# Order of splits, loads and buffers where an expansion hands over to a contraction

## The chip, the cores and the metric

The kernel runs on one core of a Trainium2 chip. Its engines have instruction queues of their own and meet through semaphores: TensorE (PE, matmuls; PEld, its weight loads), VectorE (DVE), ScalarE (ACT), GpSimd (POOL) and SyncE (SP), which here issues nearly all DMAs. The metric is the device time in microseconds of one execution.

## The reference

Linear attention with random features over 4 × 8 heads (576 tokens, 64 wide, 128 features), then two feed-forward layers on 2304 tokens of width 512:

```python
x = attention(q, k, v, omega)        # (2304, 512)
h = x @ w_in                         # 512 -> 2048
x = silu(h) @ w_out                  # 2048 -> 512
g = silu(x @ w_gate) * (x @ w_val)   # 512 -> 1536
out = g @ w_out2                     # 1536 -> 512
```

Inputs are float32, the weights are stored as float64 and converted on the chip.

## The kernel before

After the attention come four phases: up 1 (x @ w_in), down 1 (@ w_out), up 2 (gate and val), down 2. Each is a 2 × 2 block multiplication with seven products instead of eight, always in the order 1, 5, 6, 2, 7, 3, 4: the weight's quarters and their sums (A11, S1, S2, ...) against the activation's quarters and their differences (B11, T1, T2, B21, T3, B22, T4). A float32 operand is split into a high part of the matmul's type and a low part, and three matmuls (high·high, high·low, low·high) stand for one. ScalarE copies the high part, VectorE subtracts it for the low one.

An up phase runs in steps n (24 in up 1, 36 in up 2); a product of a step is 6 matmuls of 128 × 128 × 384 (L1103). ScalarE moves results between PSUM banks (L1120) and applies SiLU (L1144), VectorE adds (L1177), SyncE stores each 128 × 384 result in the DRAM tile g_d (L1129). A down phase runs over 3 blocks s of 768 tokens, seven products p and pieces k (4 in down 1, 3 in down 2); a piece is 12 matmuls (L1478). Below, (s,p,k) is such a piece.

For each piece the quarter of g is loaded by SyncE (L1311; B21 and B22 into `ra`, where up 1's weights lie, B11 and B12 into `fa`), ScalarE writes its high part (L1337), VectorE its low part (L1341), and for products 1, 5, 6 and 2 VectorE also makes the next difference in place (L1361): T1 = B12 − B11, T2 = B22 − T1, T3 = B22 − B12, T4 = B21 − T2. High and low part each take one buffer of 768 columns from the list `f_z`. In down 1 the list holds four cut from `ra` by `open_z` and one more (`gap`, given when down 1 begins); a piece's two come back when its matmuls are recorded. `open_z` may run once the weights in w_slots 4 and 5 are done with; that is so from the end of step 21 on. B21's place is that of weight slots 0 and 1, B22's that of 2 and 3; up 1's last step, 23, uses slots 2 and 3.

Down 1's weights were converted earlier and lie in DRAM (`wd_out`). For each product two or three weight pieces are loaded (L1282), ScalarE takes the high part (L1286), VectorE the low one (L1290). Pieces for products 1, 5, 6 and 2 and two of product 7 go to `ra` and `rb` while up 1 runs; product 7's last one and those of 3 and 4 go to `rc`, whose places are up 1's activations of the last block, free at its end.

The order on every engine is made when the program is built. A planner keeps a clock for each engine with its own costs, and `flush` puts urgent operations (those of the running products) first; then it takes, of several streams, the operation with the earliest start. A stream's place in the dictionary `streams` adds 0.1 us a place to that start, so it breaks near ties: `z` (loads of quarters), `wd` (weights of a down phase), `split` (a down phase's operands), `x`, `conv` (conversion of weights). `z_first(m, ...)` lists the first block's loads in the order of the names it is given.

Of the kernel before, what the change touches and what calls it, by code (L numbers as in the profile page):

```python
# [42 lines left out]
def kernel(  # L43
# [57 lines left out]
    def cut(t, o, n):  # L101
        return t[:, o : o + n]
# [43 lines left out]
    def cost(kind, n):  # L146
        a, b = fixed[kind]
        return a + b * n
# [46 lines left out]
    class Stream:  # L195
# [30 lines left out]

    streams = {
        "z": Stream(0.2),
        "wd": Stream(1.0),
        "split": Stream(1.0),  # L230
        "x": Stream(1.2, DVE=3),
        "conv": Stream(1.5, ACT=2),
    }
# [28 lines left out]
    def drain(*some):  # L262

        ready = [(o.ready(), None, o) for o in urgent]
        ready = [x for x in ready if x[0] is not None]
        for st in some or streams.values():
            o = st.best(1e9)
            if o is not None:
                ready.append((max(o.ready(), clk[o.eng]), st, o))
        if not ready:  # L270
            return False
        _, st, o = min(ready, key=lambda x: x[0])
        if st is None:
            urgent.remove(o)
            o.emit()
        else:
            st.emit(o)
        return True
# [33 lines left out]
    f_c = Free("c", [cut(fa, C_AT + i * 512, 512) for i in range(3)])  # L312
# [5 lines left out]
    w_slots = [x for x, _ in f_w.q]  # L318
    W = {}

    def conv_job(kind, i, dram=None, side=False):
        b = {}
        key = lambda *k: (kind, i, *k)
# [13 lines left out]
        def word(h, w):  # L337
            return b["r", h].bitcast(U32).rearrange("p (c w) -> p c w", w=2)[:, :, w]

        def first(h):  # L340
            def go():
                b["c", h] = c = f_c.take()

                nc.scalar.activation(c, word(h, 1).bitcast(F32), AF.Prelu, scale=2.0**-112, alpha=-(2.0**32))  # L349

            return Op("ACT", cost("ACT", 512), go, ins=[key("r", h)], outs=[key("c", h)], slots=(f_c, 1))

        def shift(h):
            def go():
# [84 lines left out]
        def store(a, z, src, ins):  # L439
# [11 lines left out]
            return Op("SP", dma_cost(P * (z - a) * 1024), go, ins=[key(*x) for x in ins], outs=[key("d", a)])  # L451

        half = [load(0), load(1), first(0), first(1), shift(0), low(0), shift(1), low(1)]
        if dram is not None:
            return [
# [50 lines left out]
    def down_job(m, i):  # L506
        k = DNK[m]
        return conv_job(
            k, i, dram=lambda a, z: wd_d[k][a:z, :, i * 256 : (i + 1) * 256].rearrange("o p c -> p o c")
        )  # L510

    def up_job_dram(k):
        return conv_job(k, 0, dram=lambda a, z: wu_d[k][:, a * 256 : z * 256])
# [386 lines left out]
    for t in spare_c:  # L900
        f_c.give(t, 0.0)
    f_sum.give(spare_sum, 0.0)
    early["conv"].extend(chain(*(conv_job("in", i, side=True) for i in range(3)), *(down_job(0, i) for i in range(3))))
    early["x"].extend(x_prep(0, 0, xr1, False, "POOL", early=True))
    def two_steps(d):
# [81 lines left out]
    for f, some in ((f_c, spare_c), (f_sum, [spare_sum])):  # L987
        n = len(f.q)
# [316 lines left out]
    def zload(m, s, n, k, after=()):  # L1305
        fp = FP[m]
        a, h = HB[n]
        f = a * fp + 2 * k

        def go():  # L1310
            nc.sync.dma_start(  # L1311
                out=ZP[n](768 * k, 768).rearrange("p (f n) -> p f n", f=2).bitcast(F32),
                in_=g_d[m][s, h, f : f + 2].rearrange("f p n -> p f n"),
            )

        return Op(
            "SP", dma_cost(2 * P * N * 4), go, ins=[("g", m, s, h, f), ("g", m, s, h, f + 1), *after], outs=[("z", m, s, n, k)],
            guard=lambda: not len(streams["conv"]),
        )
# [190 lines left out]
    def up_order(kinds, n, head, tail):  # L1510
        pairs = [(i,) for i in range(n)]
        if head:
            pairs[:3] = [(0, 1, 2)]
        if tail:
            pairs[-3:] = [(n - 3, n - 2, n - 1)]
        return [(i, k, s) for ps_ in pairs for s in range(NSB) for i in ps_ for k in kinds]
# [16 lines left out]
    def more():  # L1533

        f_c.give(extra_c)
        f_raw.give(extra_raw)
# [5 lines left out]
    seq1 = up_order(("in",), FP[0], True, True)  # L1542
# [3 lines left out]
    def z_first(m, *names):  # L1546
        return [zload(m, 0, n, k) for n in names for k in range(FP[m] // 2)]

    def open_z():

        n = len(f_w.q)
        f_w.q = deque(x for x in f_w.q if not any(x[0] is t for t in w_slots[4:]))
        assert len(f_w.q) == n - 2
        for i in range(4):
            f_z.give(cut(ra, 7424 + i * 768, 768))
# [12 lines left out]
    def hook1(n, p):  # L1568
        if n == 0 and p == CONV_P:
            streams["conv"].extend(conv1)  # L1570
        if not len(streams["x"]) and not to_come and not opened:
            opened.append(True)
            more()
        if n == len(seq1) - 6 and p == 1:
            streams["wd"].extend(wd_ops)
        if n == len(seq1) - 1 and p == 1:
            open_z()
        if n == len(seq1) - 5 and p == 1:
            streams["z"].extend(z_first(0, "B11", "B12"))
            streams["split"].extend(next(d1))  # L1580

    up_phase(0, seq1, hook1)
    while len(streams["conv"]):
        assert drain()
    assert not to_come
    streams["z"].extend(z_first(0, "B21", "B22"))

    raw2_t = []

# [54 lines left out]
    up_phase(1, seq2, hook2)  # L1644
    while len(streams["conv"]):
        assert drain()
    streams["z"].extend(z_first(1, "B21", "B22"))
    open_z()
    for _ in d2:
        pass  # L1650
# [48 lines left out]
```

## Time and profile before

| | |
|---|---|
| three runs, median (lowest to highest) | 852.97 us (851.78 to 855.28) |
| profiled execution, own time | 853.52 us |
| its span | 851.7 us |
| TensorE matmul, weight load busy | 823.9, 796.4 us |
| VectorE, ScalarE, GpSimd busy | 623.8, 552.5, 164.8 us |
| up 1 ends, down 1's first matmul | 291.9, 293.3 us |
| up 2 ends, down 2's first matmul | 722.2, 722.2 us |

Times in rows count from the span's start. A timeline merges neighbours of one line: start, length, engine, line, operation, output<-input, count, and in brackets how long the engine had been idle before it and what it waited for. A row's length reaches to the end of its last instruction; matmuls overlap, so n of them in a row take less than n times the length of one.

### The profile page before, as it was taken

How to read it: one execution, taken by the hardware profiler on the slowest of the kernel's cores; microseconds unless marked ns; L12 is line 12 of the kernel's file. 1: busy time of each engine (PE TensorE's matmuls, PEld its weight loads, DVE VectorE, ACT ScalarE, POOL GpSimd, SP SyncE). 2: the span in 40 equal slices, each digit the busy share in tenths (PEclk: the TensorE clock that was granted, in tenths of full speed). 3: DMA queues.
4: the chain of work that ended last, by engine and by line, in shares of the span. 5: the costliest groups of instructions: out<-in, count | busy, mean ns of one | idle time of the engine just before them, and what ended most of it. 6: DMA issues, size and time to landing. Idle time of an engine off the chain costs nothing.

```text
span 851.7 us, 18196 instructions
## 1 busy us (share of the span) xinstructions
PE 823.9 (97%) x6889; PEld 796.4 (93%) x6889; DVE 623.8 (73%) x1016; ACT 552.5 (65%) x1166; POOL 164.8 (19%) x204
## 2 busy tenths in 40 slices
PE   8999999999999879999998998999999999999998
PEld 7888889999899879999998998999999999899998
DVE  4888877576644687796899998584757548979783
ACT  6999878776767854455557874655556557646552
POOL 0477831044440000000000035121213010000000
PEclk9999999999999999999999999999999999999999
DMA  8579866588999865608514657462637168483602
GB/s 284 183 259 299 282 211 226 173 260 282 333 310 364 286 231 165 206 22 243 181 62 141 218 179 208 146 204 100 211 97 238 53 212 283 169 272 94 220 3 75
DMA packets 110120, 170.09 MB, mean 200 GB/s; under 512 B 9424, under 2 KB 94032, under 8 KB 110032
## 3 DMA queue, kind: packets, MB, share of 16 engines
q1 hardware_dynamic: 109808, 168.69, 60.9%
q8 instruction: 54, 0.88, 0.4%
q14 instruction: 34, 0.28, 0.1%
q10 hardware_dynamic: 224, 0.23, 0.1%
HBM read 107.02 MB, written 61.87 MB: 198 GB/s over the span
## 4 chain that ended last, share of the span: by engine, by line
PE 76%; DVE 7%; DMA 7%; issue 4%; ACT 3%; POOL 2%; SPq 0%; DVEq 0%; ACTq 0%; POOLq 0%
PE ps L1103 36%; PE ps L1478 29%; PE ps L757 4%; PE ps L801 2%; PE ps L817 2%; DMA wd_out<-fa 2%; PE ps L848 2%; DMA ra<-g_d 2%; POOL fa L382 2%; DVE fa L363 1%; DMA fa<-in_moe_w_val 1%; DVE ra L1341 1%; DMA fa<-in_moe_w_out 1%; DVE ra L429 1%; PE ps L873 1%
## 5 line engine op out<-in xcount | busy, mean ns | idle before, releaser
L382 POOL TENSOR_TENSOR fa<-fa 128x256 f32<-128x256 f32 x124 | 105.6, 866 | 506.4 <-ACT fa L1144 239.3
L1103 PE MATMUL ps<-ra 128*128 128x384 f32 x840 | 148.4, 328 | 6.1 <-ACT ps L1120 4.0
L1103 PE MATMUL ps<-rb,ra 128*128 128x384 f32 x840 | 146.3, 327 | 2.1 <-ACT ps L1120 2.1
L1103 PE MATMUL ps<-rc,ra 128*128 128x384 f32 x840 | 145.8, 326 | 1.5 <-ACT ps L1120 1.5
L1103 PEld LDWEIGHTS ps<-ra 128*128 128x128 f32 x840 | 137.6, 189 | 9.0 <-ACT ps L1120 5.8
L1103 PEld LDWEIGHTS ps<-rb,ra 128*128 128x128 f32 x840 | 137.6, 189 | 3.6 <-ACT ps L1120 3.3
L1103 PEld LDWEIGHTS ps<-rc,ra 128*128 128x128 f32 x840 | 137.8, 189 | 2.5 <-ACT ps L1120 2.4
L1120 ACT ACTIVATE ps<-ps 128x384 f32<-128x384 f32 x180 | 85.4, 477 | 67.7 <-PE ps L1103 63.4
L1177 DVE TENSOR_TENSOR fa<-fa,ps 128x384 f32<-128x384 f32 x120 | 66.2, 551 | 80.5 <-ACT ps L1120 58.0
L1337 ACT ACTIVATE ra<-fa 128x768 fp32r<-128x768 f32 x86 | 71.9, 841 | 60.4 <-PE ps L1478 43.9
L1341 DVE TENSOR_TENSOR ra<-fa,ra 128x768 fp32r<-128x768 f32 x81 | 77.4, 955 | 21.6 <-PE ps L1478 13.4
L1478 PE MATMUL ps<-ra 128*128 128x384 f32 x486 | 84.0, 332 | 6.8 <-DVE ra L1341 5.7
L1478 PE MATMUL ps<-ra,rb 128*128 128x384 f32 x516 | 89.9, 327 | 0.4 <-DVE ra L1341 0.4
L1478 PEld LDWEIGHTS ps<-ra 128*128 128x128 f32 x486 | 80.7, 192 | 9.0 <-DVE ra L1341 7.4
L1478 PE MATMUL ps<-ra,rc 128*128 128x384 f32 x482 | 83.9, 327 | 2.2 <-DVE ra L1341 2.2
L1478 PEld LDWEIGHTS ps<-ra,rb 128*128 128x128 f32 x516 | 84.5, 189 | 1.4 <-DVE ra L1341 1.0
L773 ACT ACTIVATE kq<-ps,nb 128x128 f32<-128x128 f32 x288 | 79.3, 401 | 7.8 <-DVE nb L771 7.5
L1478 PEld LDWEIGHTS ps<-ra,rc 128*128 128x128 f32 x482 | 78.9, 189 | 3.4 <-DVE ra L1341 3.2
L349 ACT ACTIVATE fa<-fa 128x512 f32<-128x512 f32 x65 | 54.0, 833 | 20.2 <-DMA fa<-in_moe_w_in 5.7
L1361 DVE TENSOR_TENSOR fa<-ra,fa 128x768 f32<-128x768 f32 x63 | 60.0, 953 | 4.4 <-DMA ra<-g_d 3.7
L1144 ACT ACTIVATE fa<-fa 128x384 f32<-128x384 f32 x84 | 43.6, 519 | 25.5 <-DVE fa L1177 25.2
L363 DVE SCALAR_TENSOR_TENSOR fa<-fa 128x512 uint32<-128x512 uint32 x65 | 56.0, 862 | 0.7
(112 smaller groups left out, 1104.5 us busy)
## 6 DMA issues: line engine op xcount, KB each, us to landing
g_d<-fa SPq DMA_DIRECT2D x168, 192.0 KB, 4.1
fa<-g_d SPq DMA_DIRECT2D x42, 384.0 KB, 5.0
ra<-g_d SPq DMA_DIRECT2D x42, 384.0 KB, 4.3
fa<-in_moe_w_out SPq DMA_DIRECT2D x28, 512.0 KB, 5.1
fa<-in_moe_w_in SPq DMA_DIRECT2D x16, 512.0 KB, 5.0
wd_out<-fa SPq DMA_DIRECT2D x12, 512.0 KB, 3.2
fa<-in_moe_w_gate SPq DMA_DIRECT2D x12, 512.0 KB, 4.0
fa<-in_moe_w_val SPq DMA_DIRECT2D x12, 512.0 KB, 5.2
```

The lines of the kernel that those rows point to most:

```text
L349: nc.scalar.activation(c, word(h, 1).bitcast(F32), AF.Prelu, scale=2.0**-112, alpha=-(2.0**32))
L363: nc.vector.scalar_tensor_tensor(c, word(h, 0), 29, c, op0=ALU.logical_shift_right, op1=ALU.bitwise_or)
L382: f(blk(f"S{n}"), blk(l), blk(r))
L773: nc.scalar.activation(e[:, g // 2, g % 2, h * M : (h + 1) * M], x[:, g, :], AF.Exp, bias=nb[:, g : g + 1])
L1103: nc.tensor.matmul(woven(ps[b][:, :N]), cut(l, j * P, P), halves(cut(r, j * N, N)), start=start and c == 0, stop=stop and c == 5, skip_gro ...
L1120: nc.scalar.activation(out() if callable(out) else out, src, AF.Copy)
L1144: nc.scalar.activation(b["t"], src, AF.Silu)
L1177: nc.vector.tensor_add(t, t if in_place else p5[n], ps[bank_][:, :N])
L1337: nc.scalar.activation(ops[s, p, k][0], src(), AF.Copy)
L1341: nc.vector.tensor_sub(l, src(), h.bitcast(F32))
L1361: (nc.gpsimd if eng == "POOL" else nc.vector).tensor_sub(z(PLACE[to]), z(PLACE.get(l, l)), z(PLACE.get(r, r)))
L1478: nc.tensor.matmul(woven(ps[BANKS[p] + e][:, :N]), cut(a, e * P, P), halves(b), start=p in FIRST and i == 0 and c == 0, stop=p in LAST and ...
```

## The change

Four edits. The stream `split` moves ahead of `wd` in the dictionary. `open_z` is called in step 22 ahead of product 5, instead of in step 23 ahead of product 1. The lists of first loads name B22 ahead of B21, in both layers. In `conv`, the first half of a conversion job may start only when no other job has had its first half without its second.

```diff
@@ -226,8 +226,8 @@
 
     streams = {
         "z": Stream(0.2),
+        "split": Stream(1.0),
         "wd": Stream(1.0),
-        "split": Stream(1.0),
         "x": Stream(1.2, DVE=3),
         "conv": Stream(1.5, ACT=2),
     }
@@ -318,6 +318,8 @@
     w_slots = [x for x, _ in f_w.q]
     W = {}
 
+    halved = []
+
     def conv_job(kind, i, dram=None, side=False):
         b = {}
         key = lambda *k: (kind, i, *k)
@@ -340,6 +342,7 @@
         def first(h):
             def go():
                 b["c", h] = c = f_c.take()
+                halved[:] = [x for x in halved if x is not b] + ([b] if h == 0 else [])
 
 
 
@@ -348,7 +351,7 @@
 
                 nc.scalar.activation(c, word(h, 1).bitcast(F32), AF.Prelu, scale=2.0**-112, alpha=-(2.0**32))
 
-            return Op("ACT", cost("ACT", 512), go, ins=[key("r", h)], outs=[key("c", h)], slots=(f_c, 1))
+            return Op("ACT", cost("ACT", 512), go, ins=[key("r", h)], outs=[key("c", h)], slots=(f_c, 1), guard=lambda: h == 1 or not halved)
 
         def shift(h):
             def go():
@@ -1573,7 +1576,7 @@
             more()
         if n == len(seq1) - 6 and p == 1:
             streams["wd"].extend(wd_ops)
-        if n == len(seq1) - 1 and p == 1:
+        if n == len(seq1) - 2 and p == 5:
             open_z()
         if n == len(seq1) - 5 and p == 1:
             streams["z"].extend(z_first(0, "B11", "B12"))
@@ -1583,7 +1586,7 @@
     while len(streams["conv"]):
         assert drain()
     assert not to_come
-    streams["z"].extend(z_first(0, "B21", "B22"))
+    streams["z"].extend(z_first(0, "B22", "B21"))
 
     raw2_t = []
 
@@ -1644,7 +1647,7 @@
     up_phase(1, seq2, hook2)
     while len(streams["conv"]):
         assert drain()
-    streams["z"].extend(z_first(1, "B21", "B22"))
+    streams["z"].extend(z_first(1, "B22", "B21"))
     open_z()
     for _ in d2:
         pass
```

Line numbers of the changed kernel are two or three higher behind the edits (L1286 becomes L1289, L1337 L1340, L1311 L1314). No matmul changes place, and no instruction of GpSimd.

ScalarE at the end of up 1, from the copy of product 5's result of step 23 (fa<-ps_82) on; ps_84<-ps_81 is the copy that up 1's last product reads. Before:

```order
L1120 ACTIVATE fa<-ps_82 128x384
L1144 ACTIVATE fa<-ps_79 128x384
L1286 ACTIVATE rb<-rb 128x768 x2
L1120 ACTIVATE ps_84<-ps_81 128x384
L1144 ACTIVATE fa<-fa 128x384 x2
L1337 ACTIVATE ra<-fa 128x768
```

Now:

```order
L1123 ACTIVATE fa<-ps_82 128x384
L1289 ACTIVATE rb<-rb 128x768
L1147 ACTIVATE fa<-ps_79 128x384
L1289 ACTIVATE rb<-rb 128x512
L1123 ACTIVATE ps_84<-ps_81 128x384
L1289 ACTIVATE rb<-rb 128x768
L1147 ACTIVATE fa<-fa 128x384
L1289 ACTIVATE rb<-rb 128x768
L1147 ACTIVATE fa<-ps_84 128x384
```

Directly ahead of the copy to ps_84 stood two weight splits of 768 columns, now one of 512 does. The split of down 1's first operand (ra<-fa), the last of the rows before, has moved to step 22, ahead of these rows.

VectorE in steps 22 and 23 of up 1, behind the low part of the first piece of product 6's weights (ra<-ra). Before:

```order
L1290 TENSOR_TENSOR ra<-ra 128x768
L1290 TENSOR_TENSOR rb<-rb 128x768
L1177 TENSOR_TENSOR fa<-fa,ps_80 128x384
L1290 TENSOR_TENSOR rb<-rb 128x512
L1290 TENSOR_TENSOR rb<-rb 128x768
L1177 TENSOR_TENSOR fa<-fa,ps_83 128x384
L1290 TENSOR_TENSOR rb<-rb 128x768
```

Now:

```order
L1293 TENSOR_TENSOR ra<-ra 128x768
L1344 TENSOR_TENSOR ra<-fa,ra 128x768
L1364 TENSOR_TENSOR fa<-fa 128x768
L1344 TENSOR_TENSOR ra<-fa,ra 128x768
L1180 TENSOR_TENSOR fa<-fa,ps_80 128x384
L1364 TENSOR_TENSOR fa<-fa 128x768
L1180 TENSOR_TENSOR fa<-fa,ps_83 128x384
L1293 TENSOR_TENSOR rb<-rb 128x768
```

Two low parts (ra<-fa,ra) and two differences T1 (fa<-fa) of down 1 now stand among up 1's sums (fa<-fa,ps), and the weights' low parts (rb) move back.

SyncE's queue around the end of up 1. ra<-g_d are the loads of B21 (the first four before) and B22 (those with waits on PE, and the one behind them), rc<-wd_out are weight pieces, g_d<-fa results of up 1. A DMAHW wait is for the DMA eight places earlier. Before:

```order
L1129 DMA g_d_64<-fa 128x384 [waits DMAHW5_49,Activation_49]
L1282 DMA rc<-wd_out 128x512 [waits DMAHW6_49,PE_49]
L1282 DMA rc<-wd_out 128x768 [waits DMAHW7_49,PE_49]
L1282 DMA rc<-wd_out 128x768 [waits DMAHW0_49]
L1129 DMA g_d_64<-fa 128x384 [waits DMAHW1_49,Activation_49]
L1129 DMA g_d_64<-fa 128x384 [waits DMAHW2_49,Activation_49]
L1311 DMA ra<-g_d_64 128x2x384 [waits DMAHW3_49]
L1311 DMA ra<-g_d_64 128x2x384 [waits DMAHW4_49]
L1311 DMA ra<-g_d_64 128x2x384 [waits DMAHW5_49]
L1311 DMA ra<-g_d_64 128x2x384 [waits DMAHW6_49]
L1311 DMA ra<-g_d_64 128x2x384 [waits DMAHW7_49,PE_49]
L1311 DMA ra<-g_d_64 128x2x384 [waits DMAHW0_49,PE_49]
```

Now:

```order
L1132 DMA g_d_64<-fa 128x384 [waits DMAHW4_49,Activation_49]
L1314 DMA ra<-g_d_64 128x2x384 [waits DMAHW5_49,PE_49]
L1314 DMA ra<-g_d_64 128x2x384 [waits DMAHW6_49,PE_49]
L1314 DMA ra<-g_d_64 128x2x384 [waits DMAHW7_49,PE_49]
L1314 DMA ra<-g_d_64 128x2x384 [waits DMAHW0_49]
L1314 DMA ra<-g_d_64 128x2x384 [waits DMAHW1_49]
L1314 DMA ra<-g_d_64 128x2x384 [waits DMAHW2_49]
L1132 DMA g_d_64<-fa 128x384 [waits DMAHW3_49,Activation_49]
L1132 DMA g_d_64<-fa 128x384 [waits DMAHW4_49,Activation_49]
L1314 DMA ra<-g_d_64 128x2x384 [waits DMAHW5_49]
L1132 DMA g_d_64<-fa 128x384 [waits DMAHW6_49,Activation_49]
L1314 DMA ra<-g_d_64 128x2x384 [waits DMAHW7_49]
```

B22's four loads and two of B21 now come ahead of the last three stores, and the weight pieces for `rc`, which stood first, come behind all eight loads.

## Rows read from the trace of the kernel before

**Rows 1.** Page, section 1: busy us, share of span, instructions.

```profile
PE 823.9 (97%) x6889; PEld 796.4 (93%) x6889; DVE 623.8 (73%) x1016; ACT 552.5 (65%) x1166; POOL 164.8 (19%) x204
```

**Rows 2.** Timeline, TensorE, 290 to 339 us: start, us, engine, line, operation, tiles, count, [wait].

```profile
290.80 1.24 PE L1103 MATMUL ps<-rc,ra 128*128 128x384 f32 x6 [0.47 <-ACT ps L1120]
...
293.33 0.43 PE L1478 MATMUL ps<-ra 128*128 128x384 f32 x1 [1.12 <-ACT ra L1337]
294.33 6.12 PE L1478 MATMUL ps<-ra 128*128 128x384 f32 x36 [0.56 <-DVE ra L1341]
300.65 2.22 PE L1478 MATMUL ps<-ra 128*128 128x384 f32 x12 [0.21 <-DVE ra L1341]
304.13 2.22 PE L1478 MATMUL ps<-ra 128*128 128x384 f32 x12 [1.26 <-DVE ra L1341]
308.33 9.89 PE L1478 MATMUL ps<-ra 128*128 128x384 f32 x48 [1.98 <-DVE ra L1341]
319.21 1.08 PE L1478 MATMUL ps<-ra 128*128 128x384 f32 x5 [0.98 <-DVE ra L1341]
320.12 18.69 PE L1478 MATMUL ps<-ra,rb 128*128 128x384 f32 x114
```

**Rows 3.** Windows: length, busy us (count) of each engine, PEclk, DMA share, GB/s.

```profile
303.00:309.00 6.00, 2.89 (x16) 2.60 (x17) 3.59 (x5) 1.81 (x3) 0.00 (x0) 1.00 1.06 380
309.00:315.00 6.00, 6.00 (x29) 6.00 (x28) 5.40 (x8) 2.83 (x4) 0.00 (x0) 0.72 0.31 120
```

**Rows 4.** Timeline, ScalarE, 279 to 297 us.

```profile
279.81 0.48 ACT L1120 ACTIVATE ps<-ps 128x384 f32<-128x384 f32 x1
...
288.80 1.57 ACT L1286 ACTIVATE rb<-rb 128x768 fp32r<-128x768 f32 x2
290.26 0.48 ACT L1120 ACTIVATE ps<-ps 128x384 f32<-128x384 f32 x1
...
296.78 0.64 ACT L1286 ACTIVATE rc<-rc 128x512 fp32r<-128x512 f32 x1 [1.66 <-DMA rc<-wd_out]
```

**Rows 5.** Timeline, VectorE, 299 to 307 us.

```profile
299.05 0.68 DVE L1290 TENSOR_TENSOR rc<-rc 128x512 fp32r<-128x512 f32 x1
...
300.52 1.82 DVE L1290 TENSOR_TENSOR rc<-rc 128x768 fp32r<-128x768 f32 x2
...
306.45 0.96 DVE L1361 TENSOR_TENSOR fa<-ra,fa 128x768 f32<-128x768 f32 x1 [2.37 <-DMA ra<-g_d]
```

**Rows 6.** Timeline, SyncE's queue: the eight loads of B21 and B22.

```profile
294.68 6.46 SPq L1311 DMA_DIRECT2D ra<-g_d  x8
```

**Rows 7.** DMA issues at 294.7 and 300.2 us: count, KB, us to landing.

```profile
ra<-g_d SPq DMA_DIRECT2D x1, 384.0 KB, 7.5
...
ra<-g_d SPq DMA_DIRECT2D x1, 384.0 KB, 9.4
```

**Rows 8.** Timeline, TensorE, 722 to 743 us, up 2 to down 2.

```profile
722.22 2.11 PE L1478 MATMUL ps<-ra 128*128 128x384 f32 x12
...
731.04 4.00 PE L1478 MATMUL ps<-ra 128*128 128x384 f32 x23 [0.69 <-DVE ra L1341]
...
735.63 0.43 PE L1478 MATMUL ps<-rb 128*128 128x384 f32 x1 [0.42 <-DVE rb L1341]
...
738.24 2.22 PE L1478 MATMUL ps<-rb 128*128 128x384 f32 x12 [0.39 <-DVE rb L1341]
740.84 0.43 PE L1478 MATMUL ps<-ra,rb 128*128 128x384 f32 x1 [0.39 <-DVE ra L1341]
```

**Rows 9.** Timeline, VectorE, 724 to 730 us.

```profile
724.25 0.95 DVE L1290 TENSOR_TENSOR rb<-rb 128x768 fp32r<-128x768 f32 x1
725.12 1.82 DVE L1290 TENSOR_TENSOR rc<-rc 128x768 fp32r<-128x768 f32 x2
726.85 0.95 DVE L1341 TENSOR_TENSOR ra<-fa,ra 128x768 fp32r<-128x768 f32 x1
729.15 0.96 DVE L1361 TENSOR_TENSOR fa<-ra,fa 128x768 f32<-128x768 f32 x1 [1.35 <-DMA ra<-g_d]
```

**Rows 10.** DMA issues at 720.45 us: the first load of B21.

```profile
ra<-g_d SPq DMA_DIRECT2D x1, 384.0 KB, 3.6
```

## The prediction

> **What bounds the kernel now.** I read the page's busy line first: TensorE's matmuls fill 97% of the span [rows 1], so a change of order can win only where TensorE stands still or runs slow. I then followed TensorE's timeline over the place that the diff moves, the change from up 1 to down 1. The reader is to see up 1's last product at 290.80 us, which waited 0.47 us for a ScalarE copy, and then six waits of down 1: 1.12, 0.56, 0.21, 1.26, 1.98 and 0.98 us, each released by a split of down 1's operands, on ScalarE (L1337) or VectorE (L1341) [rows 2]. From 320.12 us on, 114 matmuls run without a wait in 18.69 us, which is 0.1625 us each, so a piece (12 matmuls) is 1.95 us and a product of up 1 (6 matmuls) 0.975 us. The windows come next, for the clock: 6 us after the waits it is 0.72 on average, that is 1.2 GHz for part of it, and 2.4 GHz (1.00) later; in the window ahead TensorE had been busy 2.89 of 6 us [rows 3]. ScalarE, VectorE and the loads say why the operands are late [rows 4 to 7]. Last I read the second change of phase, up 2 to down 2: four waits of 0.69, 0.42, 0.39 and 0.39 us [rows 8].
>
> **The change part by part.** *Guard on the conversions' first halves.* No row of any engine ahead of up 1's step 22 changes place; I cost it at nothing.
>
> *Buffers given out earlier, splits ranked ahead of weights, at the first change.* In the sums below low part (s,p,k) is L1341's, and "late" counts from the moment at which TensorE would want it.
>
> What the old kernel loses there: the six waits are 6.11 us and the one in up 1 is 0.47. The first matmul after a wait takes 0.43 us instead of 0.33 [rows 2], 0.10 more; six times that is 0.6. The 48 matmuls from 308.33 us take 9.89 us, where 47 × 0.1625 + 0.33 = 7.97 would do: 1.9 us for the half clock. Sum 9.1 us.
>
> What becomes of each. The wait in up 1 stands behind two 768-wide weight splits, 1.57 us, ahead of copy L1120 [rows 4]. Now one 512-wide split (0.63) stands there: the copy can start when its product ends, 289.5, and ends 0.48 later, at 290.0; TensorE wants it at 290.33. So 0.47 is won. Two operand splits are added in step 22, each 0.74 in ScalarE's row. The copy that the first displaces (279.81 us before) moves to 280.56 and ends at 281.04; the product that reads it starts at 290.33 − 9 × 0.975 = 281.55: still 0.5 early. I take no loss in up 1; the bound is both splits fully exposed, 1.5 us.
>
> Down 1 then starts at 291.4 + a mark of 0.2 = 291.6 with pieces (0,1,0) and (0,1,1) ready: the waits of 1.12 and 0.56 are gone. There are five split buffers, so low part k+2 can only be written when TensorE has finished piece k: it starts about 0.2 after that (a last matmul runs 0.16 into the next piece), takes 0.95, and is 0.8 early for piece k+2. VectorE needs 0.87 for it (two in 1.82) and 0.87 for the difference L1361 behind it [rows 5]: 1.74 against TensorE's 1.95. So products 1 and 5 run without waits (0.21, 1.26 gone), if B22 is there when the first L1361 reads it, at 298.5. Before, B22's loads were the last four of eight, issued from 294.68 on [rows 6]; L1361 waited 2.37 us and started at 306.45 [rows 5], and the low part behind it was late: the wait of 1.98. Now B22's first load is issued right behind the store of step 23's first output, about 289.6 (its product ends two products before 290.33, at 288.4; then come a SiLU of 0.5 and the store's issue), its third when up 1's last product ends, 290.33 + 0.975 + 0.1 = 291.4. If each lands as slowly as the first of the burst before, 7.5 us [rows 7], the first comes at 297.1 and the third at 298.9; they are wanted at 298.5 and 302.4. No wait; 1.4 us is the cover. With no waits left TensorE is never as idle as in the window of 303 to 309, and I take the half clock's 1.9 as won too.
>
> What is late next: seven weight pieces that were split before or between products 1 and 5 now stand in products 6, 2 and 7. They cost VectorE three of 0.61 and four of 0.87 (back to back, from 0.68 and two in 1.82 [rows 5]): 5.3 us. Piece by piece: slack 0.21 where L1361 runs too, 1.08 in product 7; the low part may be 0.8 late. One 0.61 and one 0.87 in product 6, the same in product 2, the rest in product 7 push it past 0.8 four times, by 0.2, 0.5, 0.3 and 0.5: 1.5 us. ScalarE's halves of them wait for loads that come eight loads later than before: another 0.3. I take 1.8; the bounds are 0 (the slack hides all) and 5.3 (none).
>
> *SP.* B22's three first loads wait for TensorE, and the last three stores of up 1 stand behind them. Those outputs belong to block 2, whose loads start more than a block (28 × 1.95 us) later; their buffers are wanted by the copies of product 5, at 291.6 + 8 × 1.95 = 307. Nothing lost.
>
> *The second change of phase.* Old loss: waits 1.89 + four restarts × 0.10 = 2.3. VectorE did three weight pieces from 724.25 to 726.85 ahead of the first low part, then waited 1.35 for B22 at 729.15 [rows 9]. Now the low part starts at 724.25 and L1361 at 725.1. B22 takes the place of the load that landed 3.6 us after its issue at 720.45 [rows 10], at 724.1: no wait. The pieces displaced are product 7's and 3's. Product 7's first stands behind 22 VectorE instructions: 724.25 + 23 × 0.87 = 744.3, while product 7 starts at 722.22 + 12 × 1.95 = 745.6. But a low part ahead of it needs the buffer of piece 10, free at 722.22 + 11 × 1.95 = 743.7; + 0.2 + 2 × 0.95 = 745.8. So 0.2 late, and its second piece 0.1: I take 0.3, bounds 0 and 1.4 (two instructions and a half late).
>
> *Sum.* 9.1 − 1.8 + 2.3 − 0.3 = 9.3 us won. The rest of the kernel has the same order but for a few neighbours in down 1's last block, where waits of half a microsecond may move either way. The profiled execution took 853.52 us (span 851.7 and 1.8 around it): 844.2. It lay 0.55 above the median of the three runs, 852.97; on the median's scale 843.7.
>
> **The rivals.** *A, weights starve.* The slack hides none of the weight work in either change: 5.3 and 1.4 instead of 1.8 and 0.3, so 4.7 won, 848.3. For it: ScalarE waited 1.66 us for such a weight load before [rows 4]. Against: VectorE has slack in all three products.
>
> *B, B22 comes no earlier than B21.* The eight loads share the DMA engines, and if they proceed together B22's first lands with the last of them, 9.4 us after the last issue [rows 7] near 294, at 303.4, against 298.5: 4.9 lost, 1.9 for the clock again: 2.5 won, 850.5. Against: before, the first of the eight landed at 294.68 + 7.5 = 302.2 and the last at 300.16 + 9.4 = 309.6, 1.06 us apart each, so in order. The Trainium skill (DMA: Bandwidth & Descriptors, "Queues, rings and completion order") speaks for B: a copy is spread over up to 16 rings, and completion is not first in, first out per issuing engine. Here the trace, 1.06 us a load, sides with order.
>
> *C, nothing moves.* The waits are re-formed behind other instructions, only up 1's 0.47 is won: 852.5. Against: the operands' chain starts at 279.8 instead of behind up 1's end.
>
> *D, slower.* Place: ScalarE, where the low weights' first piece of product 7 stands ahead of operand split (0,6,1) in a queue in order. A load may be issued only when the eighth before it has landed, which makes generations. Piece 7.2 and its neighbour land at L and L + 1; TensorE gets its operand at L + 1 + 2 × 0.84 + 0.95 = L + 3.6 and wants it at 291.6 + 9 × 1.95 = 309.2; then the clock's 1.9 is lost again. I expect L = 303. The change wins nothing from L = 316.8 on, where 11.1 is used up. Three generations of 9.4 us from 291.9 give L = 320.1 and a loss of 16.4: 5.3 slower, 858. Against: in the old burst only the second generation took that long.
>
> **How the numbers follow.** A difference under 0.5% (4.3 us, about what a measurement of this kernel can tell from none) counts as the same. Forecast 0.66, A 0.15, B 0.08, C 0.07, D 0.04. The forecast's own range is 840.5 (all costs nothing: 11.4 won, 841.6, and a microsecond of scatter) to 847. The range for 8 in 10 takes in A with scatter: 840.0 to 849.0. Faster than 848.7: the forecast, two thirds of A, a fifth of B, 0.78; the same: the rest of A and B and C, 0.18; slower 0.04.
>
> **What would show it.** Right: up 1's last copy without a wait ahead of its product; the first down matmul within 0.5 us of up 1's end; no wait for B22's load on VectorE at either change; clock 1.00 throughout; TensorE's waits in products 6, 2 and 7 of block 0 below 3 us together. Wrong: ScalarE waiting for a weight load (A, D), L1361 waiting for a load (B), a clock drop near 310 (any). The prediction fails if the seven weight pieces cost TensorE more than 5 us, or if up 1's copies come late for its own products.

## The result, and the profile after

The changed kernel takes 842.12 us (median of six runs, 840.66 to 843.65); the kernel before took 852.66 beside it. The ratio is 0.9873, with a 95% interval of 0.9852 to 0.9893: 1.3% faster, against a forecast of 843.7. The profiled execution is the slowest of the six, 843.65 us.

Its page, section 1 (busy us, share of the span, instructions), answers [rows 1]:

```profile
PE 821.9 (98%) x6889; PEld 795.9 (95%) x6889; DVE 626.4 (74%) x1016; ACT 552.7 (66%) x1166; POOL 163.8 (19%) x204
```

The page hides the gain, since busy times hardly moved. TensorE's timeline at the change from up 1 to down 1 shows it, against [rows 2] (lines of the changed kernel are 3 further down: L1106 is L1103, L1481 is L1478):

```profile
273.65 19.66 PE L1106 MATMUL ps<-rc,ra 128*128 128x384 f32 x120
293.15 0.34 PE L1409 MATMUL ps<-ra 128*128 128x384 f32 x1
293.33 18.69 PE L1481 MATMUL ps<-ra 128*128 128x384 f32 x114
311.85 7.26 PE L1481 MATMUL ps<-ra,rb 128*128 128x384 f32 x43
319.29 8.24 PE L1481 MATMUL ps<-ra,rb 128*128 128x384 f32 x48 [0.18 <-DVE ra L1344]
327.71 4.00 PE L1481 MATMUL ps<-ra,rb 128*128 128x384 f32 x23 [0.18 <-DVE ra L1344]
```

Up 1 ends without a wait, the single matmul between the phases (L1409, the prediction's "mark") starts at 293.15, and down 1's first 114 matmuls run through at 0.1625 us each. Where six waits stood in down 1, the timeline marks two, of 0.18, further on. The windows that answer to [rows 3] show no drop of the clock (PEclk, the first of the last three values, is 1.00 in both):

```profile
303.00:309.00 6.00, 6.00 (x39) 6.00 (x38) 5.93 (x8) 4.26 (x6) 0.00 (x0) 1.00 1.04 407
309.00:315.00 6.00, 6.00 (x39) 5.87 (x37) 6.00 (x9) 6.00 (x11) 0.00 (x0) 1.00 0.10 37
```

ScalarE's timeline, against [rows 4]: two of the operand's high parts (L1340) now stand inside up 1, and one 512-wide weight split stands directly ahead of up 1's last copy (L1123 at 291.46).

```profile
281.82 0.83 ACT L1340 ACTIVATE ra<-fa 128x768 fp32r<-128x768 f32 x1
...
283.34 0.83 ACT L1340 ACTIVATE ra<-fa 128x768 fp32r<-128x768 f32 x1
...
290.94 0.63 ACT L1289 ACTIVATE rb<-rb 128x512 fp32r<-128x512 f32 x1
291.46 0.49 ACT L1123 ACTIVATE ps<-ps 128x384 f32<-128x384 f32 x1
...
306.91 0.84 ACT L1289 ACTIVATE rc<-rc 128x768 fp32r<-128x768 f32 x1 [0.35 <-DMA rc<-wd_out]
```

VectorE's timeline, against [rows 5] and, in its last row, [rows 9]. The first difference that reads B22 (L1364) starts at 300.44 and at 718.33 with no wait; it waited 2.37 and 1.35 us before. A low part of the late weights (L1293) now stands between the operand's own at 313.06 and 317.41:

```profile
300.44 0.96 DVE L1364 TENSOR_TENSOR fa<-ra,fa 128x768 f32<-128x768 f32 x1
...
313.06 0.95 DVE L1293 TENSOR_TENSOR rc<-rc 128x768 fp32r<-128x768 f32 x1
...
317.41 0.95 DVE L1293 TENSOR_TENSOR rc<-rc 128x768 fp32r<-128x768 f32 x1
318.28 0.95 DVE L1344 TENSOR_TENSOR ra<-ra 128x768 fp32r<-128x768 f32 x1
...
718.33 0.96 DVE L1364 TENSOR_TENSOR fa<-ra,fa 128x768 f32<-128x768 f32 x1
```

SyncE's queue, against [rows 6], and the issue of B22's first load at 291.49 us with its time to landing, against [rows 7]:

```profile
291.49 3.75 SPq L1314 DMA_DIRECT2D ra<-g_d  x6
```

```profile
ra<-g_d SPq DMA_DIRECT2D x1, 384.0 KB, 3.1
```

At the second change of phase, the four waits of [rows 8] are gone: TensorE does not wait between 690 and 760 us.

For a ledger I add, over all matmuls of a stretch, by how much more than 0.1625 us the next one started after it. At the first change (278 to 345 us) TensorE lost 10.30 us before and 1.19 after, at the second (690 to 760) 2.96 and 0: 12.1 won. The profiled execution shows 853.52 − 843.65 = 9.87, because the same matmul of up 1's step 22 came 2.0 us later than in the profile before, with the same instructions in the same order ahead of it. This is scatter between executions: in the fourteen profiles of this study, the first matmul of step 22 starts between 276.2 and 279.5 us. The medians are 10.5 apart; of the 1.6 us between that and the ledger no run here shows more than that it lies within this scatter.

### The profile page after: what moved, and what is told of

Its sections match the earlier page's. It is cut to its first block, busy times and chain, and to the rows that moved or that the text cites. A ratio compares the mean times of both kernels' runs of the same rounds, so it can differ in the third digit from the quotient of the medians.

```text
span 841.9 us, 18188 instructions
## 1 busy us (share of the span) xinstructions
PE 821.9 (98%) x6889; PEld 795.9 (95%) x6889; DVE 626.4 (74%) x1016; ACT 552.7 (66%) x1166; POOL 163.8 (19%) x204
## 4 chain that ended last, share of the span: by engine, by line
PE 76%; DMA 6%; DVE 6%; ACT 5%; issue 3%; POOL 3%; SPq 0%; ACTq 0%; DVEq 0%; POOLq 0%
PE ps L1106 35%; PE ps L1481 31%; PE ps L760 4%; POOL fa L385 3%; PE ps L804 2%; DMA wd_out<-fa 2%; PE ps L820 2%; PE ps L851 2%; ACT kq L776 2%; DMA g_d<-fa 1%; DMA fa<-in_moe_w_val 1%; DVE fa L366 1%; DMA x_d<-fa 1%; DVE ra L432 1%; PE ps L876 1%
## 5 line engine op out<-in xcount | busy, mean ns | idle before, releaser
L1106 PE MATMUL ps<-ra 128*128 128x384 f32 x840 | 148.6, 328 | 7.0 <-ACT ps L1123 4.9
L1106 PE MATMUL ps<-rb,ra 128*128 128x384 f32 x840 | 146.3, 327 | 1.6 <-ACT ps L1123 1.6
L1106 PEld LDWEIGHTS ps<-ra 128*128 128x128 f32 x840 | 137.6, 189 | 10.1 <-ACT ps L1123 7.0
L1106 PE MATMUL ps<-rc,ra 128*128 128x384 f32 x840 | 145.8, 326 | 1.1 <-ACT ps L1123 1.0
L1106 PEld LDWEIGHTS ps<-rb,ra 128*128 128x128 f32 x840 | 137.6, 189 | 3.2 <-ACT ps L1123 3.1
L1106 PEld LDWEIGHTS ps<-rc,ra 128*128 128x128 f32 x840 | 137.8, 189 | 2.0 <-ACT ps L1123 2.0
L1123 ACT ACTIVATE ps<-ps 128x384 f32<-128x384 f32 x180 | 85.6, 480 | 66.2 <-PE ps L1106 62.5
L1340 ACT ACTIVATE ra<-fa 128x768 fp32r<-128x768 f32 x86 | 72.1, 842 | 60.3 <-PE ps L1481 51.1
L1344 DVE TENSOR_TENSOR ra<-fa,ra 128x768 fp32r<-128x768 f32 x81 | 77.4, 956 | 19.1 <-PE ps L1481 11.1
L1481 PE MATMUL ps<-ra,rb 128*128 128x384 f32 x516 | 90.6, 327 | 0.4 <-DVE ra L1344 0.4
L1481 PEld LDWEIGHTS ps<-ra,rb 128*128 128x128 f32 x516 | 84.4, 189 | 2.0 <-DVE ra L1344 1.5
L1481 PE MATMUL ps<-ra,rc 128*128 128x384 f32 x482 | 83.9, 327 | 2.3 <-DVE ra L1344 2.3
L1481 PEld LDWEIGHTS ps<-ra,rc 128*128 128x128 f32 x482 | 78.9, 189 | 3.5 <-DVE ra L1344 3.4
L1481 PE MATMUL ps<-ra 128*128 128x384 f32 x486 | 80.4, 326 | 0.0
L1481 PEld LDWEIGHTS ps<-ra 128*128 128x128 f32 x486 | 79.2, 189 | 0.0
L1364 DVE TENSOR_TENSOR fa<-ra,fa 128x768 f32<-128x768 f32 x63 | 60.1, 954 | 0.7
```

The source lines that it names most:

```text
L1106: nc.tensor.matmul(woven(ps[b][:, :N]), cut(l, j * P, P), halves(cut(r, j * N, N)), start=start and c == 0, stop=stop and c == 5, skip_gro ...
L1123: nc.scalar.activation(out() if callable(out) else out, src, AF.Copy)
L1340: nc.scalar.activation(ops[s, p, k][0], src(), AF.Copy)
L1344: nc.vector.tensor_sub(l, src(), h.bitcast(F32))
L1364: (nc.gpsimd if eng == "POOL" else nc.vector).tensor_sub(z(PLACE[to]), z(PLACE.get(l, l)), z(PLACE.get(r, r)))
L1481: nc.tensor.matmul(woven(ps[BANKS[p] + e][:, :N]), cut(a, e * P, P), halves(b), start=p in FIRST and i == 0 and c == 0, stop=p in LAST and ...
```

## The experiments

The change has three parts with an effect (the guard moves no instruction: the program without it is the same, on every engine). **R**: operand splits ranked ahead of weight splits. **L**: B22 loaded ahead of B21. **G**: the split buffers given out in up 1's last step but one. My theory: TensorE waited for operand splits that stood behind weight splits, so R is most of it. Rivals: L, or G. "Lost" is the ledger's, at the first and the second change of phase, in us; the difference is that of the medians to the kernel before, run on the same chip.

| kernel | median | difference | ratio, 95% interval | lost, first | lost, second |
|---|---|---|---|---|---|
| before | 852.7 to 853.4 | | | 10.30 | 2.96 |
| R + L + G (the change) | 842.12 | −10.5 | 0.9852 to 0.9893 | 1.19 | 0 |
| R | 842.64 | −10.5 | 0.9848 to 0.9889 | 1.73 | 1.35 |
| L | 849.32 | −3.9 | 0.9926 to 0.9965 | 7.96 | 1.65 |
| G | 854.23 | +1.1 | 1.0004 to 1.0034 | 11.89 | 2.35 |
| L + G | 850.69 | −2.5 | 0.9956 to 0.9979 | 7.88 | 1.65 |
| R + G | 842.59 | −10.8 | 0.9849 to 0.9885 | 1.80 | 1.30 |
| R + L | 842.00 | −11.4 | 0.9840 to 0.9878 | 1.72 | 0 |
| R in the up phases only | 848.17 | −5.0 | 0.9929 to 0.9959 | 6.79 | 1.99 |
| R in the down phases only | 850.30 | −2.8 | 0.9954 to 0.9983 | 9.58 | 0 |

**The ranking alone (R).**

```
     streams = {
         "z": Stream(0.2),
+        "split": Stream(1.0),
         "wd": Stream(1.0),
-        "split": Stream(1.0),
```

> Only the ranking of the splits is changed: operand splits go ahead of weight splits; B21 is still loaded ahead of B22, and the split buffers are still given out in up 1's last step. Theory (the splits' place in ScalarE's and VectorE's row is the cause of most of the gain): both high parts of unit 1 still come before up 1's end, so five of the six waits of the first change of phase go; B22.0 comes fifth in the row of loads, some 4 us later than in the changed kernel (landings about 1.06 us apart), which leaves a wait of 0 to 1.5 us; at the second change of phase up to 3 us stay. Time 842.7 + 0.5 to 4, that is 843 to 847. Rival 1 (the order of the loads is the cause): only little moves, 850 or more. Rival 2 (the early giving-out is the cause): 852 or more.

842.64: the whole gain, as far as the intervals tell, and a little more than expected. The wait on B22 that I allowed for at the first change did not come. With the ranking, SyncE's queue has all eight loads of B21 and B22 ahead of the third weight group, of which three stood ahead of them before. B22.0, fifth in the row, was issued at 291.01, landed 6.7 us later, at 297.7, and its reader stood at 298.59: 0.9 us of cover. At the second change it does come late. VectorE's and then TensorE's timeline of this kernel:

```profile
720.48 0.96 DVE L1361 TENSOR_TENSOR fa<-ra,fa 128x768 f32<-128x768 f32 x1 [2.61 <-DMA ra<-g_d]
```

```profile
722.36 4.00 PE L1478 MATMUL ps<-ra 128*128 128x384 f32 x23 [1.08 <-DVE ra L1341]
```

**The order of the loads alone (L).**

```
-    streams["z"].extend(z_first(0, "B21", "B22"))
+    streams["z"].extend(z_first(0, "B22", "B21"))
...
-    streams["z"].extend(z_first(1, "B21", "B22"))
+    streams["z"].extend(z_first(1, "B22", "B21"))
```

> Only the order of the loads is changed: B22 ahead of B21 at both changes of phase. Theory of the ranking: the waits on B22 shrink (2.37 us on VectorE at the first change, 1.35 us at the second), the waits on the unit's high parts, which still stand behind weight splits, stay: 2 to 4.5 us won of 10.5, time 848 to 850.5. Rival 1 (the order of the loads is the cause): 842 to 844. Rival 2 (the early giving-out): 852 to 853.

849.32, inside the theory's range. The waits on the high and low part at up 1's end stay; TensorE's timeline of this kernel shows them, and the windows a clock of 0.56 (half speed, 1.2 GHz, for most of 3.9 us) right after them:

```profile
294.74 0.43 PE L1478 MATMUL ps<-ra 128*128 128x384 f32 x1 [1.12 <-ACT ra L1337]
295.74 9.75 PE L1478 MATMUL ps<-ra 128*128 128x384 f32 x48 [0.56 <-DVE ra L1341]
306.36 10.02 PE L1478 MATMUL ps<-ra 128*128 128x384 f32 x60 [0.88 <-DVE ra L1341]
```

```profile
293.00:295.70 2.70, 1.05 (x5) 0.50 (x3) 2.23 (x3) 2.56 (x6) 0.00 (x0) 1.00 0.46 150
295.70:299.60 3.90, 3.87 (x13) 3.87 (x14) 2.98 (x4) 2.04 (x4) 0.00 (x0) 0.56 0.91 220
```

**The early giving-out alone (G).**

```
-        if n == len(seq1) - 1 and p == 1:
+        if n == len(seq1) - 2 and p == 5:
             open_z()
```

> Only the point is changed at which the split buffers of up 1's last operand are given out: one step earlier. Theory of the ranking: the first high and low part of unit 1 come into up 1 and their waits go (some 2.5 us), but the second high part still stands behind up 1's end, and B22 is loaded behind three weight pieces and all of B21, so that its wait grows by about as much: 849 to 853. Rival 1 (the order of the loads): 852 to 853. Rival 2 (the early giving-out is the cause): 842 to 844.5.

854.23, just above the range and slower than before. The first part of the expectation holds: down 1's first matmuls start at once. Then TensorE stands for 8 us. In order, this kernel's TensorE, VectorE, SyncE's queue, and the issue of B22's first load:

```profile
292.96 10.75 PE L1478 MATMUL ps<-ra 128*128 128x384 f32 x61
311.86 10.92 PE L1478 MATMUL ps<-ra 128*128 128x384 f32 x53 [8.15 <-DVE ra L1341]
```

```profile
309.98 0.96 DVE L1361 TENSOR_TENSOR fa<-ra,fa 128x768 f32<-128x768 f32 x1 [5.94 <-DMA ra<-g_d]
```

```profile
293.23 1.34 SPq L1282 DMA_DIRECT2D rc<-wd_out  x3
294.67 0.86 SPq L1129 DMA_DIRECT2D g_d<-fa  x2
295.62 2.02 SPq L1282 DMA_DIRECT2D rc<-wd_out  x3
297.68 5.36 SPq L1311 DMA_DIRECT2D ra<-g_d  x6
```

```profile
ra<-g_d SPq DMA_DIRECT2D x1, 384.0 KB, 7.8
```

Six weight loads, where there were three before, now stand ahead of B21 and B22. B22.0 is issued at 302.0 and lands 7.8 us later, at 309.9, where its reader starts. So two waits at up 1's end were traded for one that is longer than both, because a third queue moved. The windows show what else it cost: the clock is at 0.50 when TensorE starts again, which then runs 13 matmuls in 4 us, where 0.1625 us each would make about 24:

```profile
308.00:312.00 4.00, 0.14 (x1) 0.14 (x1) 2.02 (x3) 0.00 (x0) 0.00 (x0) 0.50 0.92 325
312.00:316.00 4.00, 4.00 (x13) 4.00 (x14) 3.97 (x5) 1.16 (x2) 0.00 (x0) 0.50 0.02 7
```

**Loads and giving-out without the ranking (L + G).** Edit: the two diffs above together.

> The order of the loads and the early giving-out are changed, the ranking is as before. Theory of the ranking: the first high part's wait goes and B22 comes earlier, the second high part and the low part behind weight splits still make TensorE wait; at the second change of phase only B22's wait goes: 845.5 to 849.5. Rival (the ranking does nothing that the other two don't do): 842 to 843.5.

850.69, a little above the range: the same stop, shorter by the four loads of B21 that no longer stand ahead of B22 (B22.0 is issued at 297.00 and lands at 304.8):

```profile
306.79 3.90 PE L1478 MATMUL ps<-ra 128*128 128x384 f32 x12 [3.84 <-DVE ra L1341]
```

**The ranking with one of the others (R + G, R + L).** Edits: the first and the third diff; the first and the second.

> The ranking and the early giving-out, without the change in the order of the loads (B21 first at both changes of phase). Theory (the ranking gives the gain; the loads' order is worth the one wait at the second change, 1.35 us of TensorE in the run with the ranking alone): 842.7 to 844, with one wait of about 1.1 us near 722 us. Rival (B22's order is needed at the first change too, once the operand parts come early): a wait on B22 there of 2 us or more, 845 or more.

842.59: the wait at the second change is there (1.30 lost). At the first change VectorE does wait for B22, but only 0.99 us, and TensorE loses 0.15 by it. The rival, which asked for 2 us or more and 845, falls. VectorE's timeline of this kernel:

```profile
298.07 0.96 DVE L1361 TENSOR_TENSOR fa<-ra,fa 128x768 f32<-128x768 f32 x1 [0.99 <-DMA ra<-g_d]
```

> The ranking and the order of the loads, with the split buffers given out in up 1's last step as before. Theory (the early giving-out does nothing for the time once the operand's splits outrank the weights'): 841.5 to 842.7, no wait at the second change of phase, the first change at 1.0 to 1.3 us of lost TensorE time. Rival (it is needed for the high parts to be early): a wait of 1 us or more at up 1's end, 843.5 or more.

842.00, with no wait at the second change. The first change loses 1.72, more than the 1.0 to 1.3 expected; 0.52 of it is a wait in up 1 that both kernels with R and G lack. With R + G other small waits in down 1 take its place (1.80 lost, against 1.73 with R alone). So in the traces L is worth 1.4 us on top of R and 1.9 on top of R + G; G is worth nothing on top of R and 0.5 on top of R + L. The intervals of all four kernels with R overlap, so in the times neither can be told from nothing.

**Half of the ranking.** A function that puts the streams into the old or the new order is called before and after each up phase:

```
+    def rank(*names):
+        q = {k: streams[k] for k in names}
+        streams.clear()
+        streams.update(q)
...
+    rank(*NEW)
     up_phase(0, seq1, hook1)
+    rank(*OLD)
```

(for the up phases; the other way round for the down phases, and the same at up 2).

> The ranking alone, and only while the up phases are planned; from the end of up 1 and of up 2 on, weight splits go first again as before. It keeps the high and low parts of unit 1 inside up 1 and puts the third weight group's low parts (7.2, 3.x, 4.x) back among the low parts of product 6. If the start of the operand's splits in up 1 is what counts: 843 to 845, the waits at the first change below 2 us in all. If the weights' place in the down phase counts as well: 2 to 5 us of waits in product 6 and 2 to 3 at the second change, 846 to 850.

848.17, in the range for the second case. TensorE starts down 1 at once, but in product 6 ScalarE makes two weights' high parts ahead of the operand's, VectorE makes three weights' low parts at a stretch between two of the operand's, and TensorE waits three times. This kernel's ScalarE, VectorE and TensorE (lines are 7 further down than before: L1293 is L1286, L1297 is L1290, L1344 is L1337, L1348 is L1341, L1485 is L1478):

```profile
308.40 1.56 ACT L1293 ACTIVATE rc<-rc 128x768 fp32r<-128x768 f32 x2
309.87 0.83 ACT L1344 ACTIVATE ra<-fa 128x768 fp32r<-128x768 f32 x1
```

```profile
311.61 2.42 DVE L1297 TENSOR_TENSOR rc<-rc 128x768 fp32r<-128x768 f32 x3
```

```profile
310.75 0.43 PE L1485 MATMUL ps<-ra 128*128 128x384 f32 x1 [1.34 <-ACT ra L1344]
311.75 1.08 PE L1485 MATMUL ps<-ra 128*128 128x384 f32 x5 [0.56 <-DVE ra L1348]
...
315.82 19.33 PE L1485 MATMUL ps<-ra,rb 128*128 128x384 f32 x107 [1.86 <-DVE ra L1348]
```

> The ranking alone, and only from the end of each up phase on, off again while up 2 is planned. The high parts of unit 1 come after up 1's end as before (waits of 1.30 and 0.83 us of TensorE there, 0.74 at the copy), the weights' low parts come behind the operand's. If the place of the weights in the down phase is what counts: 843 to 845.5. If the start in up 1 counts as well: 3 us of waits at up 1's end and up to 2.5 us on B22, which is still loaded last behind three weight pieces: 846 to 849.

850.30, above the range: the waits at up 1's end, then 2.32 us for a low part behind B22, whose loads still stand behind three weight loads, and the half clock twice (each time about ten matmuls start 0.16 us too late):

```profile
293.94 0.43 PE L1485 MATMUL ps<-ra 128*128 128x384 f32 x1 [1.11 <-ACT ra L1344]
294.94 11.70 PE L1485 MATMUL ps<-ra 128*128 128x384 f32 x60 [0.56 <-DVE ra L1348]
308.96 10.49 PE L1485 MATMUL ps<-ra 128*128 128x384 f32 x53 [2.32 <-DVE ra L1348]
```

The halves win 5.0 and 2.8, the whole 10.5: a wait removed at up 1's end comes back later if the low parts or B22 are late for their own reasons. At the second change, the ranking in the down phase loses nothing in its profile, though B22 is loaded last there too: VectorE waited 1.13 us for it, not 2.61 as with R.

**A further step: VectorE in down 1's last block.** There TensorE still loses 3.9 us (430 to 475 us), with low parts standing among VectorE's work for up 2's first operand. Differences of that operand on GpSimd, which is idle there; first for its first unit, then for the second too (the same edit in `x_prep(1, 1, ...)`):

```
-                streams["x"].extend(x_prep(1, 0, raw2, True, "DVE"))
+                streams["x"].extend(x_prep(1, 0, raw2, True, "POOL"))
```

> The changed kernel, and the eight differences of the next operand (up 2's, first unit), which lie in down 1's last block on VectorE (8 x 0.47 us, among the low parts that TensorE waits for), made on GpSimd, which is idle there (its own 128x384 differences took 1.0 us each elsewhere). If those differences are what the low parts stand behind, TensorE's 3.6 us of waits in that block shrink by 1.5 to 3: 839 to 841. If the low parts stand behind the next operand's low parts or behind ScalarE's high parts, nothing moves: 842. If the slower differences delay up 2's first step, 843 or more.

> As the run before, and the differences of up 2's second unit on GpSimd too (eight more, some 3.8 us off VectorE in the early up 2). By the same reasoning 0 to 1 us beyond it: 838.5 to 841; if TensorE's waits at 494 to 527 us are on ScalarE's copies alone, the same as the run before.

848.35 and 850.57 (ratios to before 0.9920 to 0.9950 and 0.9944 to 0.9974): 6 and 8 us slower than the change, a plain miss. (The first expectation did allow for 843 or more, but by a delay of up 2's first step; the loss is in down 1's last block.) TensorE loses 10.02 and 12.29 us in that block. Its longest wait, with GpSimd and VectorE beside it, in the first of the two kernels:

```profile
446.78 1.41 PE L1481 MATMUL ps<-ra,rc 128*128 128x384 f32 x7 [3.49 <-DVE ra L1344]
```

```profile
437.06 2.87 POOL L622 TENSOR_TENSOR fa<-ra,fa 128x384 f32<-128x384 f32 x2 [22.75 <-ACT ra L1340]
439.89 3.00 POOL L622 TENSOR_TENSOR fa<-ra 128x384 f32<-128x384 f32 x2
442.86 2.58 POOL L622 TENSOR_TENSOR fa<-ra,fa 128x384 f32<-128x384 f32 x2
```

```profile
437.31 3.43 DVE L1344 TENSOR_TENSOR ra<-fa,ra 128x768 fp32r<-128x768 f32 x2
440.67 2.64 DVE L600 TENSOR_TENSOR ra<-fa,ra 128x384 fp32r<-128x384 f32 x2
443.23 2.62 DVE L600 TENSOR_TENSOR ra<-ra 128x384 fp32r<-128x384 f32 x2
```

The same VectorE instructions in the changed kernel, with GpSimd idle:

```profile
435.06 1.02 DVE L600 TENSOR_TENSOR ra<-ra 128x384 fp32r<-128x384 f32 x2
...
446.62 1.82 DVE L1344 TENSOR_TENSOR ra<-ra 128x768 fp32r<-128x768 f32 x2
```

3.43 for 1.82 and 2.6 for 1.02: while GpSimd works, VectorE's instructions, all with two inputs, take 1.9 and 2.6 times as long. Alone, VectorE's six would take 1.82 + 2 × 1.02 = 3.9 us and GpSimd's six about 6 (an estimate: four such differences earlier in the kernel before took 1.00 each); together they took 8.8 (437.06 to 445.85). That is nearly one after the other. VectorE's six end 4.6 us later by it (8.5 us for 3.9), and about ten matmuls behind TensorE's longest wait each start 0.16 us too late (the clock is 0.66 from 447 to 452 us). By their size, these two make up the 6.1 us that TensorE loses in this block beyond the change.

**The same work earlier.** In the changed kernel up 2's first operand is begun one or two products earlier (product 6 or 5 in place of 2), on VectorE:

```
-            if p == 2:
+            if p == 6:
                 streams["x"].extend(x_prep(1, 0, raw2, True, "DVE"))
```

> The changed kernel with up 2's first operand prepared one product earlier in down 1's last block (from product 6 on instead of product 2), all on VectorE. If VectorE has room there, the waits of 3.6 us in that block shrink by 1 to 2.5 us: 840 to 841.5. If it only moves them forward, 842.

> The same, two products earlier (from product 5 on). With room on VectorE the waits of that block shrink by 1 to 3 us: 839.5 to 841.5; if it only moves them forward, 842.

841.48 and 842.43 (intervals of the ratio 0.9848 to 0.9888 and 0.9857 to 0.9891): no gain that can be told from none. The first time lies just inside the range for room on VectorE, but its trace doesn't bear that out: TensorE loses 3.90 us in that block, as in the change. Two products earlier the waits move forward (4.79). None of these versions beats the change by more than its interval.

## Why the prediction was right

**The place and the mechanism: shown.** It put the loss on operand splits behind weight splits at the two changes of phase. Undoing only the ranking (L + G) gives back 8 of the 10.5 us, making only the ranking keeps all of them, within the intervals. By the ledger this holds for the first change of phase; at the second, R and L each leave about half of the loss (1.35 and 1.65 of 2.96), and both together nothing.

**Up 1.** The copy without a wait and the two added high parts at no cost: both as predicted.

**Products 1 and 5 without a wait, down 1 within 0.5 us of up 1's end:** 114 matmuls in 18.69 us, 0.18 us behind the mark.

**B22.** No wait, as predicted, but with far more cover: it landed at 294.6, 5.8 us ahead of its reader, where the sum had 1.4. I took 7.5 us to landing from a burst that stood behind weight loads; issued behind stores alone it took 3.1. What was wrong in the step is whose merit this is: at the first change B22 is early mainly because the ranking sends the third weight group's loads behind it. R alone, with B21 first, has no wait there either, though it is close: 0.9 us of cover, and with G beside it VectorE waits 0.99. Rival B, that order does not matter because the loads finish together, falls by the same run: the fifth load landed 6.7 us after its issue, in its turn.

**The seven displaced weight pieces.** Predicted: four slips of 0.2, 0.5, 0.3 and 0.5 us and 0.3 for ScalarE, 1.8 in all. The trace has four, of 0.10, 0.44, 0.17 and 0.44 (at 315, 319, 323 and 328 us), 1.19 in all (with 0.02 behind the mark). ScalarE did wait for a weight load, 0.35 us at 306.91, which the prediction called a sign of rivals A or D; it cost TensorE nothing.

**The second change of phase.** 2.3 lost before and 0.3 after was predicted; 2.96 and 0 is in the ledger. B22's first load landed at 717.1, 1.3 us ahead of its reader, where the sum had 1.0. Product 7's weight pieces came in time; their 0.3 lay between bounds of 0 and 1.4.

**The term that was mis-sized: what a wait costs.** The sum counted a wait's idle time and 0.10 for the first matmul after it. The rows give 0.16 more. The run that starts at 311.85 ends at 319.11; without a wait the next would start 0.16 before that end (as at 331.55, where 327.71 + 4.00 − 0.16), but it starts at 319.29: 0.34 late, with an idle time of 0.18 shown. Seven waits at the first change and four at the second make 11 × 0.16 = 1.8 us, which is the difference between 9.1 + 2.3 and the ledger's 10.30 + 2.96. It was the larger part of the 2.8 us by which the sum of 9.3 fell short of 12.1; the slips, 1.2 for 2.1, are most of the rest. Two small errors of the sum cancel: with up 1's there are seven waits and so seven restarts, not six, and the 9.89 us from which the half clock's 1.9 is taken hold one of them. The medians show 10.5, which is 1.2 more than the sum. That the forecast lies so near is in part luck: the ledger's 12.1 would have made 840.6, and what made the medians differ by less was in no sum.

**The rival on the slower side** (weights so late that ScalarE's row blocks) had the right shape and the wrong load. Its weight pieces landed from 305.9 us on, against 316.8 as the point from which it decides. (With the clock's 1.9, which D counts, that point is 314.7: L + 3.6 − 309.2 + 1.9 = 11.1; nothing hangs on it.) But G alone is slower than before through the same queue: there it is B22 that stands behind weights.

## What to carry to other kernels

Where one queue order feeds several engines in order, rank what the next stage waits for ahead of what it needs a product later, in the old stage and in the new one: half of it is worth less than half. Ask of an edit to one engine's order what it does to the order of the loads, since this was a part of the gain (R) and all of the loss (G). Before moving work to an idle engine, look for rows of both engines busy at once.

## What the runs showed of the hardware that was not expected

- GpSimd and VectorE held each other up, with the rows above: 8.8 us for work of 3.9 and, by estimate, 6. The Trainium skill says so (SBUF — State Buffer, "SBUF: two separate sides"): the two share a pair of SBUF ports under an exclusive lock, and an instruction of VectorE with two SBUF inputs is blocked by one of GpSimd that reads SBUF. The trace agrees in the main (one after the other would make 9.9 us), and I should have weighed it ahead of the run.
- The same pair of waits (1.1 and 0.56 us at up 1's end) was followed by ten matmuls at half clock in two profiles (L, R in the down phases) and by none in the profile before, whose matmuls from 294.33 on ran at full clock [rows 2]. The 1.6 to 1.7 us that the half clock cost there are thus not a fixed part of a wait's price.
- A wait of 0.18 us costs TensorE 0.44: 0.16 of overlap between neighbouring matmuls and 0.10 at the restart, beside the idle time that the profile shows.
